# First scores, first loads and first mixing rewritten in a blockwise attention and MLP-mixer kernel

## The chip, the cores and the metric

The kernel runs on one core of one Trainium2 chip. A core has a matrix engine (TensorE, PE), a vector engine (VectorE, DVE), a scalar engine (ScalarE, ACT), a general one (GpSimd, POOL) and a queue engine (SyncE, SP). Each takes its own instructions strictly in the order of its queue and waits on semaphores for the others. Loads and stores are issued by an engine and carried out by 16 DMA engines which all the queues share. The metric is the time of one execution in microseconds (us).

## The reference

There are 8 batches of 8 heads, 576 positions and 64 elements per head; all inputs and outputs are float32.

```python
scores = np.matmul(q, k.transpose(0, 1, 3, 2)) / np.sqrt(64)
scores = np.where(i // 64 >= j // 64, scores, -1e9)         # causal in blocks of 64
attn = exp(scores - max); attn = attn / (sum(attn) + 1e-9)
x = concat_heads(attn @ v)                                  # (8, 576, 512)
h = np.maximum(x^T @ w_tok1, 0) @ w_tok2                    # mixes positions, 576 -> 256 -> 576
u = x + h^T
out = u + np.maximum(u @ w_ch1, 0) @ w_ch2                  # mixes channels, 512 -> 1536 -> 512
```

## The kernel before

**How work is ordered.** The kernel first describes its work as operations, `P.add(engines, cost, emit, ...)`. An operation is a small group of instructions of one engine (a group of matmuls into one PSUM bank, a load, an exponential) and gets the next number. The string `ORDER` (from line 100) then lists all of them by hand: a number, the letter of the engine (T = PE, A = ACT, D = DVE, P = POOL, S = SP), and the letters of the PSUM banks that the operation takes (a to h; s and t are the pair banks of the first scores). `placed()` emits them in that order, so that ORDER is, engine by engine, the queue that runs. Costs and priorities beside an operation play no part any more. Semaphores between the engines follow from the tiles that are read and written.

**A batch.** Four heads of one k or q (a "first" and a "second" half of the heads, hg 0 and 1) are one load of 128 partitions by 1152 elements. From the second batch on, and for all values and weights, POOL's queue loads them and casts them to bf16 on the way (L418 for k and q, L468 for the values). DVE turns them with 32x32 stream transposes, two per load (L442). PE then makes scores (L568), ACT their exponentials (L587 for the first batch, L774 for others), POOL, DVE or ACT copy tails (L596) and clear blocks (L601), PE multiplies by the values (L618, L638), and DVE divides by the row sums (L644). That gives x. Token mixing is `token_up` (L809, relu at L795 or L797), then for every 128 positions products with w_tok2 (L904), a DVE add of x (L919) which gives u as rows, four PE transposes (L991) and an evacuation of them (L1007 by ACT, L1009 by DVE), which gives u as columns (`uT`). Channel mixing is `channel_up` (L1032) and `channel_down_fast` (L1366), a product of blocks with fewer multiplications, which needs sums and differences of weight blocks made by DVE (`weight_sums`, L1318, for w_ch2; `up_weight_sums`, L1063, for w_ch1), and which ends in `fold`: DVE adds the residual u (L1412) and SyncE stores the rows (L1457). The last 64 positions of all batches are put together at the end as one more batch.

**The start of the first batch.** `load_qk(0, 0)` brings the first heads in four halves, (0, 9) and (9, 18) of 18 groups of 64 elements: both halves of k and the first of q are loaded by SyncE as float32 into `stage` (space in `gT`) and cast to bf16 by ACT (L400) or DVE (L402); the second half of q comes in two casting loads by POOL's queue, groups 9 to 14 and 14 to 18 (L437). `load_qk(0, 1)` brings the second heads by POOL in two halves for q and two for k. `init_tiles` fills constants (L344): ones and zeros of the two value tiles, the zero rows of w_tok1 and of its odd copy `w1o_sb`. `raise_clock` gives PE matmuls on zeros while nothing else is there: 11 of 512 columns and up to 110 of 256 columns (ORDER takes them with T).

**The order of POOL's loads before.** Two q pieces; second heads' q, then k, in halves; batch 1's k of the first heads; five pieces of the first heads' values; batch 1's q; one piece of the second heads' values; w_tok2; four more value pieces with batch 1's second k between them; w_tok1 in three; batch 1's second q; one piece of w_ch1; batch 2's first q; the other seven of w_ch1 (L502); batch 2's first k; the values of batch 1; batch 2's second k and q; w_ch2 in three (L511).

**First batch's mixing before.** `first_uT` makes the columns of u directly. For each 128 channels, four matmuls of x with the identity (L842) put x^T into a bank and two matmuls of 512 columns (L857) add the mixing; one evacuation by ACT or DVE (L872, L874) gives `uT`. The rows of u, which `fold` needs, are made later by `turn`: four times four matmuls of `uT` with the identity (L1388) and a cast (L400 or L402).

```python
    ORDER = """
    13S 22P 24P 5P 9D 2D 3P 16S 44Ta 12P 19S 10P 4P 30P 14D 15D 17A 32P 1D 26P 18D 20A 28P 0A 45Tb 23D 25D 21D 252P 46Tb
```

Of the kernel before, what the change touches and what calls it, by code (L numbers as in the profile page):

```python
# [27 lines left out]
class Plan:  # L28
# [19 lines left out]
    def __init__(self):  # L48
        self.ops = []
        self.free = {}  # L50
# [4 lines left out]
    def add(  # L55
        self, engines, cost, emit, deps=(), prio=0.0, take=(), give=(), xfer=None, mode=0, at=0.0,
        urgent=0, until=1e9, quick=False, stick=False,
# [10 lines left out]
        o.n = len(self.ops)  # L68
        self.ops.append(o)
# [5 lines left out]
    def placed(self):  # L75
# [21 lines left out]
        assert all(o.n in done or o.until < 1e9 for o in self.ops)  # L97
# [3 lines left out]
    13S 22P 24P 5P 9D 2D 3P 16S 44Ta 12P 19S 10P 4P 30P 14D 15D 17A 32P 1D 26P 18D 20A 28P 0A 45Tb 23D 25D 21D 252P 46Tb  # L101
    47Tb 48Tb 49Ta 50Ta 37P 51Ta 52Ta 53Ta 54Ta 55Ta 56Ta 35P 57Ta 7D 174Tst 175T 34P 195A 58Ta 59Ta 60Ta
    61Ta 196A 62Ta 38P 197D 63Ta 31D 64Ta 65Ta 66Ta 176A 199Tt 36P 177A 178D 67Ta 179D 68Ta 33D 69Ta 255P 70Ta 200A
    180Ts 27D 198P 71Ta 72Ta 40P 73Ta 181A 29D 182Tt 157P 74Ta 75Ta 76Ta 183A 77Ta 201Ts 43P 78Ta 79Ta 80Ta 253D
    202A 42P 214Tt 254D 188Tb 189T 41P 215A 184Tc 11D 233Ts 6D 190D 191D 258P 192Td 211Ta 234A 220Tt 216P 256D 39P
    185T 257D 221A 81Tb 218Ts 155P 212D 213D 207Tb 235D 208T 186D 219A 158P 187D 237Tt 193D 209D 156P 203Ta 210D
    204T 238A 194D 239Ts 261P 205D 206D 164P 8D 240A 236D 269Tcbda 424P 271A 163P 281Tefgh 270A 166P 259D 273A 217D
    226Tb 283A 227T 284A 222Tc 223T 228D 241Ta 242T 282A 229D 165P 249Tf 224D 245Tg 285A 225D 162P 246T 230Tb 243D
    244D 339Tc 159P 250D 231D 232D 337Ta 251D 247D 161P 340A 260D 272A 276Tbfeh 338D 348Tc 262D 160P 278A 349T 263D
    345Ta 280A 346T 248D 277A 341Td 350D 421P 301Tgbfh 274D 347D 264P 343Tc 342D 303A 275D 351Ta 304A 265P 352T 344D  # L110
    305A 425D 354Td 355T 302A 313Tcbfh 279A 356D 306P 387Tg 353A 267P 426D 384Td 315A 388T 266P 316A 404Ta 385T 317A
    268P 408Tb 314A 381Te 386D 405A 416Tf 427P 409D 390Tc 389A 307P 391T 333D 430P 372Td 392A 308Tabhg 167P 373T
    311A 334D 382T 168P 310A 369Tc 309A 370T 169P 417A 375Tb 335D 434P 312A 378Ta 379T 383A 433P 366Th 374A 367T
    422D 371A 436P 400Td 423D 376T 380A 289Tc 377A 295Ta 290D 298Tf 368A 291D 330Tb 296D 401A 297D 292Tc 299D 286Tg
    331D 332D 438Tadeh 300D 287D 293D 288D 324Tb 440A 294D 357Tf 325D 439A 321Tc 326D 363Tg 428D 442A 364T 322D 441A
    323D 450Tbdah 431D 365A 318Tc 429D 454A 358T 453A 319D 327Te 432D 360Tg 451A 320D 361T 452A 328D 329D 482Tcabh
    362A 443D 359D 502Te 444P 483A 435P 393D 485A 604P 484A 504Td 503A 437P 170D 486A 470Tcbag 595P 505A 171D 601P
    473A 445Tfehd 471A 172D 514Ta 448A 508Tc 472A 173D 515A 512Th 506Tb 446A 509D 510Ta 474A 513D 397Tcf 447A 475P
    507D 449A 476P 394D 598P 477Tbghe 398A 403Td 395D 480A 479A 511D 481A 493Th 396D 520Ta 478A 490Tg 518Te 521A
    494D 407T 406D 519A 495D 597D 464Ta 596D 455Te 461Th 410D 458Tb 399T 465D 491D 456D 457D 462D 459D 466D 411T  # L120
    463D 600D 402D 496Ta 522Te 412D 516Th 413T 523A 497D 599D 419S 517A 460D 762P 492D 499Te 414D 759P 467Tb
    612Thgcd 498D 526D 415T 336D 615A 616A 614A 530Tca 613A 487Td 500D 468D 469D 531Tg 533A 501D 617P 527D 545Thb
    532A 418D 618P 536T 611P 548A 524Te 488D 489D 534Tg 537A 525D 610P 551T 528D 535A 624Tdecf 605D 608P 552A 538T
    606D 628A 607P 540T 529D 627A 539D 678Th 626A 609P 603D 625A 549Tc 602D 679A 619Tdfge 541D 550A 546Th 622A 760D
    553T 623A 763D 543T 620A 547D 676Tg 621A 761D 544A 644Tdehf 542D 926P 677A 554D 555T 647A 764D 560Tag 648A 556D
    561Tc 929P 563A 680Th 557D 765P 562A 684Tf 681D 645A 566T 558T 685D 646A 564Tc 567A 649D 559D 651Tdhef 650P 565A
    768P 638Ta 653A 635Tb 772P 639D 568T 652A 640D 570T 636D 654A 637D 686Ta 569D 655A 656Tbdhe 571D 641Tc 660A 687D
    629Tf 659A 573T 642D 630D 689S 643D 632Ta 658A 631D 682Te 572D 657A 788Tcfdh 633D 634D 574A 673Tb 683D 790A
    670Ta 674D 789A 664Tg 688S 675D 671D 579Tef 672D 791A 665D 792A 666D 769D 783Tbagc 580A 667Td 784A 661Th 668D
# [45 lines left out]
    1473T 1472D 1381A 1411D 1477S 1534T 1531D 1474D 1574Tbc 1570D 1554Tag 1535D 1575A 1571D 1475T 1555A 1550D 1537D  # L175
    1576T 1539D 1540T 1476D 1551D 1478S 1580T 1552D 1542T 1541D 1547S 1578Td 1546S 1543D 1560T 1572D 1544T 1573D
    1581D 1553D 1558Th 1561D 1545D 1564T 1579D 1548S 1549A 1559D 1584T 1565D 1582T 1577D 1585D 1566T 1589A 1583D
    1556T 1588A 1567D 1562T 1569S 1557D 1586T 1563D 1568S 1587D 1590S
"""


# [1385 lines left out]
```

## Time and profile before

| | us |
|---|---|
| median of 3 runs | 284.15 |
| lowest and highest | 283.65, 284.55 |
| the profiled execution | 284.69 |
| its span, first to last instruction | 282.9 |
| PE: first scores | 8.30 |
| ACT: exponentials of the first batch | 9.06 to 21.32 |
| PE: first channel-up product | 32.14 |
| PE: first scores of the third batch | 43.69 |
| PE: first down product | 55.75 |

A row of the profile's timeline or of its chain of waits reads "start, length, engine, line, operation, output<-input, count", and in brackets the idle time of the engine before it with what ended it. `x9` stands for nine instructions drawn together. A row of the groups of instructions has busy time and mean nanoseconds of one behind the first bar. In the DMA view a queue's row gives packets, MB and its packets' time as a share, and an issue's row the size of one and the median time from issue to landing. q0 is POOL's queue, q1 SyncE's. All times count from the start of the span; 1.8 us of the execution lie outside of it.

The granted clock of PE has a mean of 1.0 over the span.

### The profile page before, as it was taken

The page shows a single profiled execution, that of the slowest core. Times are in us where ns is not written, and L with a number is a line of the kernel's source. Part 1 is how long each engine was busy: PE and PEld are TensorE (multiplying, and loading weights), DVE is VectorE, ACT ScalarE, POOL GpSimd, SP SyncE. Part 2 cuts the span into 40 slices and gives each one's busy share as a digit, 9 for nine tenths or more (in the row PEclk, how much of TensorE's full clock was granted, in tenths as well). Part 3 has the DMA queues.
Part 4 walks back from the last instruction along what each step waited for, and adds up shares of the span by engine and source line. Part 5 has one row for each costly group of instructions (what it writes and reads, how often), then busy time and mean ns, then how long its engine had stood idle before and what let it go on. Part 6 is the DMA issues. An engine that isn't in the chain of part 4 may idle for free.

```text
span 282.9 us, 9352 instructions
## 1 busy us (share of the span) xinstructions
PE 275.3 (97%) x3982; PEld 204.0 (72%) x3982; DVE 238.9 (84%) x515; ACT 179.2 (63%) x331; POOL 72.7 (26%) x126
## 2 busy tenths in 40 slices
PE   7899999999999999999999999999999999999994
PEld 3466556588776788986877658756789876568884
DVE  3688669999889998999998979859896997579984
ACT  3798788953998856897879866274533744652200
POOL 8895870511631351063232221000000000000000
PEclk9999999999999999999999999999999999999999
DMA  7999999954979492999598594100044502200157
GB/s 163 160 178 192 202 190 206 152 92 86 142 87 139 87 150 56 250 109 170 66 118 139 56 188 60 70 10 19 0 84 95 196 0 76 75 1 2 74 151 224
DMA packets 64890, 31.95 MB, mean 113 GB/s; under 512 B 53200, under 2 KB 55888, under 8 KB 64848
## 3 DMA queue, kind: packets, MB, share of 16 engines
q0 software_dynamic: 44896, 17.49, 53.6%
q1 hardware_dynamic: 19520, 13.21, 18.2%
q8 instruction: 31, 0.51, 0.7%
q10 hardware_dynamic: 432, 0.66, 0.7%
q14 instruction: 11, 0.09, 0.1%
HBM read 35.85 MB, written 9.44 MB: 160 GB/s over the span
## 4 chain that ended last, share of the span: by engine, by line
PE 87%; DMA 4%; ACT 3%; POOL 3%; DVE 1%; issue 1%; POOLq 0%; DVEq 0%
PE late L1366 23%; PE mm L1105 8%; PE mm L1232 7%; PE mm L1366 7%; PE late L1232 6%; PE mm L568 6%; PE late L1105 6%; DMA qk_sb<-in_k_dram 4%; PE mm L618 4%; PE mm L809 3%; PE mm L904 2%; PE late L904 2%; PE late L618 2%; PE mm L1032 2%; ACT e_sb L774 2%; PE late L809 2%
## 5 line engine op out<-in xcount | busy, mean ns | idle before, releaser
L774 ACT ACTIVATE e_sb<-mm 128x512 bf16<-128x512 f32 x82 | 46.6, 606 | 13.1 <-PE late L568 9.4
L774 ACT ACTIVATE e_sb<-late 128x512 bf16<-128x512 f32 x86 | 48.5, 609 | 9.0 <-PE late L568 8.2
L442 DVE STREAM_TRANSPOSE qk_sb<-qk_sb 128x288 int32<-128x288 int32 (+1 forms) x65 | 41.8, 694 | 4.9 <-DMA qk_sb<-in_q_dram 1.8
L468 POOL DMA_DIRECT2D vals<-in_v_dram x45 | 36.9, 832 | 4.5 <-PE mm L618 2.4
L1366 PEld LDWEIGHTS <-gT 128*128 128x128 bf16 x336 | 32.0, 98 | 5.6 <-issue 0.4
L1366 PEld LDWEIGHTS <-sums 128*128 128x128 bf16 x324 | 31.3, 98 | 5.3 <-issue 0.4
L568 PEld LDWEIGHTS <-qk_sb 32*64 32x64 bf16 (+1 forms) x1152 | 19.0, 103 | 14.8 <-issue 11.1
L568 PE MATMUL mm<-qk_sb 32*64 32x64 bf16 (+7 forms) x504 | 26.9, 277 | 0.1
L618 PEld LDWEIGHTS <-e_sb 128*128 128x128 bf16 x640 | 23.1, 97 | 5.3 <-issue 2.2
L568 PE MATMUL late<-qk_sb 32*64 32x64 bf16 (+7 forms) x504 | 26.2, 283 | 0.6 <-issue 0.3
L1366 PE MATMUL late<-wd_sb,gT 128*128 128x256 bf16 x168 | 20.7, 273 | 0.0
L1366 PE MATMUL late<-wd_sb,sums 128*128 128x256 bf16 x168 | 20.6, 273 | 0.0
L1105 PEld LDWEIGHTS <-ws_sb 128*128 128x128 bf16 x192 | 18.2, 98 | 3.1 <-issue 0.9
L618 PE MATMUL mm<-vals,e_sb 128*128 128x65 bf16 x450 | 19.8, 193 | 0.5 <-DMA vals<-in_v_dram 0.3
L644 DVE TENSOR_TENSOR x_sb<-mm,rinv 128x256 bf16<-128x256 f32 x45 | 18.7, 422 | 1.3
L1412 DVE TENSOR_TENSOR o_sb<-late,u_sb 128x512 f32<-128x512 f32 x22 | 15.0, 684 | 3.6 <-PE late L1366 3.6
L1232 PEld LDWEIGHTS <-ws_sb 128*128 128x128 bf16 x120 | 11.7, 98 | 8.6 <-issue 0.2
L1105 PEld LDWEIGHTS <-wc_sb 128*128 128x128 bf16 x144 | 15.3, 114 | 1.5 <-issue 0.4
L1366 PE MATMUL late<-wc_sb,gT 128*128 128x256 bf16 x132 | 16.2, 273 | 0.0
L596 POOL COPY vals<-e_sb 128x256 bf16<-128x256 bf16 (+1 forms) x11 | 4.3, 393 | 39.7 <-ACT e_sb L774 39.6
L400 ACT COPY mm<-late 128x512 f32<-128x512 f32 (+1 forms) x16 | 9.1, 570 | 8.1 <-PE late L1232 5.4
L795 ACT ACTIVATE gT<-mm 128x512 bf16<-128x512 f32 x21 | 12.6, 616 | 1.9 <-PE mm L1105 0.9
(198 smaller groups left out, 630.7 us busy)
## 6 DMA issues: line engine op xcount, KB each, us to landing
out_dram<-o_sb SPq DMA_DIRECT2D x19, 256.0 KB, 3.0
qk_sb<-in_k_dram POOLq DMA_DIRECT2D x14, 288.0 KB, 6.0
qk_sb<-in_q_dram POOLq DMA_DIRECT2D x14, 288.0 KB, 5.9
vals<-in_v_dram POOLq DMA_DIRECT2D x28, 128.0 KB, 4.5
out_dram<-o_sb SPq DMA_DIRECT2D x7, 512.0 KB, 3.8
wc_sb<-in_moe_w_ch_dram POOLq DMA_DIRECT2D x8, 192.0 KB, 7.5
wc_sb<-in_moe_w_ch_dram POOLq DMA_DIRECT2D x3, 512.0 KB, 10.5
vals<-in_v_dram POOLq DMA_DIRECT2D x15, 64.0 KB, 5.3
```

The lines of the kernel that those rows point to most:

```text
L442: nc.vector.transpose(dst[:, 0:S, :] .rearrange("p s e -> p (s e)") .bitcast(I32) .rearrange("p (a k) -> p k a", k=NB)[:, k0:k1], raw2.bit ...
L468: nc.gpsimd.dma_start(out=t[128 - p : 128, J, hs, 0:64], in_=src)
L568: nc.tensor.matmul(out=home(n)[rows, c : c + w], lhsT=bar[r, 0] if j is None else kT[i][r, keys, par], rhs=bar[r, 1] if j is None else qT[ ...
L618: nc.tensor.matmul(out=u[:, I, 0:65], lhsT=e[:, h, c : c + 128], rhs=vt[:, J, head, 0:65], start=(J == 0), stop=(J == I),)
L644: nc.vector.tensor_tensor(out=xt[:, 0:4, 64 * head : 64 * head + 64], in0=u[:, :, 0:64], in1=ri[:, 0:4].to_broadcast([128, 4, 64]), op=MULT,)
L774: nc.scalar.activation(dst, bank_of(x), EXP, scale=scale)
L795: nc.scalar.activation(dst, src, RELU)
L809: nc.tensor.matmul(out=ps, lhsT=w1_sb[:, c, tt : tt + 255 : 2], rhs=xt[:, c, cols], start=(c == 0), stop=False)
L1105: nc.tensor.matmul(out=bank_of(bank)[:, 256 * o_ : 256 * o_ + 256], lhsT=x(o_, m), rhs=y[:, :, m, :], start=opens, stop=m == 1, skip_group ...
L1232: nc.tensor.matmul(out=bank_of(bank)[:, 128 * c : 128 * (c + step)], lhsT=x(m), rhs=y[:, c : c + step, m, :], start=opens, stop=m == 1, sk ...
L1366: nc.tensor.matmul(out=bank_of(bank)[:, 256 * i : 256 * i + 256], lhsT=x[:, kk, 128 * i : 128 * i + 128], rhs=y[:, kk], start=first and i ...
L1412: nc.vector.tensor_tensor(out=dst, in0=src, in1=other, op=ADD)
```

## The change

It has these parts.

1. The second half of the first heads' q is loaded by SyncE as float32 and cast by ACT, as the other three halves are, and turned by one stream transpose, not two.
2. The second heads' q and k of the first batch come in one POOL load each, cast on the way, not in two.
3. Two fills move from DVE to POOL, ahead of its loads: the zero rows of the second value tile and those of `w1o_sb`.
4. POOL's loads have another order: second heads' q, then k; the five value pieces of the first heads; batch 1's k, then q, of the first heads; the five value pieces of the second heads; w_tok1 in three; w_tok2; batch 1's k, then q, of the second heads; w_ch1 in eight; batch 1's values; batch 2's k and q of the first heads; k and q of the second; w_ch2 in three.
5. The first batch's mixing goes by rows, as in the other batches: for each half of the channels and each 256 positions, four matmuls of 256 columns, a DVE add of x (now u as rows), four transposes, an evacuation. `turn` goes, since the rows are there. These operations are numbered from 2000 on.
6. The first 24 of PE's fillers on zeros are two matmuls of 128 columns, not one of 256.
7. The first batch's upper half of rows is stored by one DMA, not two.
8. The early part of ORDER is written anew. Operations from 25 on have a number one lower. From the second batch's token mixing on (about 55 us), each engine's operations are the same in the same order, with other PSUM banks. Earlier, besides the above: two relus of the first batch's token_up pass from DVE to ACT, one of the second batch's from ACT to DVE, four evacuations of the first channel-up swap between ACT and DVE, and some tail copies between POOL and DVE.

```diff
 def add(..., later=False):
-        o.n = len(self.ops)
+        if later:
+            o.n, self.later = self.later, self.later + 1
+        else:
+            o.n, self.count = self.count, self.count + 1
 ...
 ORDER = """
-    13S 22P 24P 5P 9D 2D 3P 16S 44Ta 12P 19S 10P 4P 30P 14D 15D 17A 32P 1D 26P 18D 20A 28P 0A 45Tb 23D 25D 21D 252P 46Tb
-    47Tb 48Tb 49Ta 50Ta 37P 51Ta 52Ta 53Ta 54Ta 55Ta 56Ta 35P 57Ta 7D 174Tst 175T 34P 195A 58Ta 59Ta 60Ta
+    13S 5P 9D 2D 3P 16S 43Ta 12P 19S 22S 10P 4P 6P 11P 29P 14D 15D 17A 1D 25P 18D 20A 23A 0A 44Tb 21D 24D 36P 45Tb 46Tb
+    47Tb 48Ta 49Ta 34P 50Ta 51Ta 52Ta 53Ta 54Ta 55Ta 33P 56Ta 7D 173Tst 174T 37P 194A 57Ta 58Ta 59Ta 60Ta 195A 61Ta 35P
 ...
-    WARM, KEEP = 11, 110
+    WARM, KEEP, HALVED = 11, 110, 24
 ...
         for i in range(2):
+            fill("POOL", ("v", i), -1e6 + i, (v1[i][0:64, 4, :, :], 0.0))
             fill(
                 ("POOL", "DVE")[i], ("v", i), (-1e6, -40)[i],
-                (v1[i][0:64, 4, :, :], 0.0),
 ...
-        fill("DVE", "w1", -1e5 + 3, (w1o_sb[0:64, :], 0.0))
+        fill("POOL", "w1", -9e5 + 1, (w1o_sb[0:64, :], 0.0))
 ...
-            if not first:
+            if b or hg:
 ...
-            edges = (0, 9, 18) if not (first and n) or hg else (0, 9, 14, 18)
+            edges = (0, 9, 18)
             for f, (k0, k1) in enumerate(zip(edges, edges[1:])):
-                if first and not hg and n + f < 2:
+                if first and not hg:
 ...
-    def first_uT(x_done, a_done, w2_ready):
+    def first_uT(a_done, w2_ready):
+        xt, at, ut = x_sb[0], aT[0], u_sb[0]
+        done, rows = [], {}
+        P.count += 3 * NDM
+        for f in range(2):
+            cols = slice(256 * f, 256 * f + 256)
+            for p in range(2):
+                def emit(o, p=p, cols=cols, bank=bank):
+                    for i in range(2):
+                        for t in range(NDT):
+                            si = 2 * p + i
+                            nc.tensor.matmul(
+                                out=bank_of(bank)[:, 256 * i : 256 * i + 256],
+                                lhsT=w2_sb[:, t, 128 * si : 128 * si + 128], rhs=at[:, t, cols],
+                                start=i == 0 and t == 0, stop=t == NDT - 1, skip_group_check=i > 0,
+                            )
 ...
+                    nc.vector.tensor_tensor(
+                        out=ut[:, 2 * p : 2 * p + 2, cols],
+                        in0=bank_of(bank).rearrange("p (t c) -> p t c", c=256),
+                        in1=xt[:, 2 * p : 2 * p + 2, cols], op=ADD,
+                    )
 ...
+                    ps = bank_of(bank).bitcast(BF16)[:, 0:512]
+                    for i in range(2):
+                        for m in range(2):
+                            nc.tensor.transpose(
+                                ps[:, 256 * i + 128 * m : 256 * i + 128 * m + 128],
+                                ut[:, 2 * p + i, 256 * f + 128 * m : 256 * f + 128 * m + 128], ident,
+                            )
 ...
+                    dst = uT[0][:, 2 * p : 2 * p + 2, 2 * f : 2 * f + 2, :]
 ...
+        return done, rows
 ...
-                rows_done = u_done if b else [turn(row, col)] if residual else []
+                if b == 0:
+                    P.count += 2 * residual
+                    rows_done = [u_done[row, col]] if residual else []
+                else:
+                    rows_done = u_done
 ...
-                    step = 1 if row == 0 else nt
+                    step = 1 if row == 0 and b else nt
```

More of the change, by code (lines that the diff above doesn't have):

```diff
@@ L48, in __init__ @@
     def __init__(self):
-        self.ops = []
+        self.ops = {}
+        self.count, self.later = 0, 2000
         self.free = {}
@@ L56, in add @@
         self, engines, cost, emit, deps=(), prio=0.0, take=(), give=(), xfer=None, mode=0, at=0.0,
-        urgent=0, until=1e9, quick=False, stick=False,
+        urgent=0, until=1e9, quick=False, stick=False, later=False,
     ):
@@ L435, in load_qk @@
                 elif first:
-                    def emit_load(o, k0=k0, k1=k1, hbm=hbm, raw2=raw2):
-                        nc.gpsimd.dma_start(out=raw2[:, D * k0 : D * k1], in_=hbm[:, D * k0 : D * k1])
-                    loads = [P.add("POOL", 0.69 if not hg and f == 1 else 0.55, emit_load, (), -1e4 + n + 4 * hg, xfer=0.084 * (k1 - k0) + 0.3 * (not hg and f == 1))]
+                    P.count += f
                 def emit(o, raw2=raw2, dst=dst, k0=k0, k1=k1):
@@ L892, in token_mix @@
             ]
[L893 removed]
+            done, u_done = first_uT(a_all, w2_ready)
             prio = 0.5
```

255 lines of the change are left out of this document (117 added, 138 removed).

## The prediction

> **What bounds the kernel now.** I read the page's shares first, then the chain of work that ended last, then the timeline of each engine up to 60 us, and last the DMA view in short windows, since the change touches nothing later: from the second batch's token mixing on (about 55 us) both orders name the same operations in the same sequence on every engine.
>
> ```profile
> PE 275.3 (97%) x3982; PEld 204.0 (72%) x3982; DVE 238.9 (84%) x515; ACT 179.2 (63%) x331; POOL 72.7 (26%) x126
> PE 87%; DMA 4%; ACT 3%; POOL 3%; DVE 1%; issue 1%; POOLq 0%; DVEq 0%
> 6.63 6.33 DMA qk_sb<-in_k_dram
> 15.86 6.03 DMA qk_sb<-in_k_dram
> 21.98 0.72 DVE qk_sb L442
> 45.01 1.57 ACT e_sb L774 x3
> ```
>
> The first two rows are TensorE's busy share and the chain by engine: late in the run PE alone sets the end, so whatever PE gains by 60 us should stay gained. The other four are rows of the chain (start, length, what): before 23 us it runs through POOL's loads, not through PE, and from 45 to 52 us through ScalarE's exponentials. So the early part has three limits in turn, and a saving on PE alone is not automatically a saving.
>
> **The start.** The first scores need all of the first k and q.
>
> ```profile
> gT<-in_k_dram SPq DMA_DIRECT2D x2, 288.0 KB, 3.0
> gT<-in_q_dram SPq DMA_DIRECT2D x1, 288.0 KB, 5.1
> q1 hardware_dynamic: 213, 0.43, 93.3%
> q1 hardware_dynamic: 97, 0.20, 53.9%
> q0 software_dynamic: 133, 0.07, 51.0%
> 6.82 0.67 ACT L400 CAST qk_sb<-gT 128x576 bf16<-128x576 f32 x1 [1.77 <-DMA gT<-in_q_dram]
> 6.60 1.65 DVE L442 STREAM_TRANSPOSE qk_sb<-qk_sb 128x160 int32<-128x160 int32 x3 [0.80 <-DMA qk_sb<-in_q_dram]
> 8.30 0.51 PE L568 MATMUL sc<-qk_sb 32*64 32x192 bf16 x28 [1.53 <-DVE qk_sb L442]
> ```
>
> Rows one and two: issue to landing of SyncE's loads; the k halves took 3.0 us, the q half 5.1. Rows three to five are the queues (packets, MB, share) in 2.50-3.75 us and 3.75-5.00 us: alone, SyncE's queue moved 0.43 MB in 1.25 us, 0.34 MB per us; once POOL's queue joined it fell to 0.20 MB. With POOL's q pieces gone, SyncE's four halves (1.18 MB) have the engines to themselves until POOL's next load moves. By 3.75 us it has moved 0.58 MB, so the other 0.60 MB need about 1.75 us, to 5.5, and I allow 0.5 us to landing (the two k halves' last bytes moved near 3.9 us, their cast began at 4.37): third half 5.15, fourth 6.0. Two ScalarE casts of 0.67 us end at 6.7, one stream transpose of 0.7 (the last of the three in row seven) at 7.45, instead of 8.25 now. PE starts its scores at 7.45: **0.85 us earlier**. Bounds: if the last half takes 3.2 us from its issue at 2.1 it is 1.4 us earlier; if both q halves queue as the one does now (6.82, then 0.68 more) the scores start at 8.95, 0.65 later. The middle is nearer the undisturbed rows, so I take it.
>
> ```profile
> 9.06 7.09 ACT L587 ACTIVATE e_sb<-sc 128x384 bf16<-128x384 f32 x9 [1.47 <-PE sc L568]
> 16.39 4.93 ACT L587 ACTIVATE e_sb<-sc 128x1024 bf16<-128x1024 f32 x5 [0.23 <-PE sc L568]
> ```
>
> From 9.06 to 21.32 ScalarE runs batch 0's exponentials with one gap of 0.23 us, so the 0.85 us passes through to 20.45, if the second heads' k and q are there.
>
> **POOL's queue.** POOL drops two q pieces and loads the second heads' q and k in two issues, not four, but gains two fills ahead of them.
>
> ```profile
> 1.25 1.24 POOL L437 DMA_DIRECT2D qk_sb<-in_q_dram  x2 [0.80 <-POOLq L1551]
> 4.52 1.08 POOL L437 DMA_DIRECT2D qk_sb<-in_q_dram  x2
> 7.15 3.65 POOL L468 DMA_DIRECT2D vals<-in_v_dram  x5
> L344 POOL MEMSET vals<- 64x528 bf16 x1 | 0.5, 532 | 0.1
> L344 POOL MEMSET w_sb<- 64x256 bf16 x1 | 0.6, 591 | 0.1
> 13.24 0.54 POOL L479 DMA_DIRECT2D w_sb<-in_moe_w_tok_dram  x1 [0.70 <-DMA qk_sb<-in_k_dram]
> ```
>
> The two q issues of the first row (1.24 us) go, fills of 0.53 and 0.59 us come, so the second heads' q is issued near 4.5 as now (4.52); two issues of 0.54 us fewer let the values follow near 5.5 instead of at 7.15, the more so as batch 1's k goes behind them. The last row is a back-pressure: the fifteenth load waited for the seventh (6.63 + 6.33 = 12.96), so POOL keeps eight loads in flight and from 12 us on is paced by landings. Through that queue I count 288 KB of bf16 per k or q load: k of batch 1's second heads now lands at 21.88 and its transpose (21.98) sits in DVE's queue ahead of the clear that PE's head products wait for:
>
> ```profile
> 21.37 0.63 PE L568 MATMUL late<-qk_sb 32*128 32x512 bf16 x8 [0.30 <-ACT e_sb L587]
> 22.28 0.45 PE L618 MATMUL mm<-vals,e_sb 128*128 128x65 bf16 x9 [0.28 <-DMA vals<-in_v_dram]
> 22.93 0.81 PE L618 MATMUL mm<-vals,e_sb 128*128 128x65 bf16 x21 [0.21 <-DVE e_sb L601]
> ```
>
> In the new order the values and w_tok1 come first (the values near 18 us instead of 22.3) and the clears stand before that transpose, so the 0.35 us before each of the last two rows goes: **0.7 us**. What is late next: that k itself. Behind the values, w_tok1 and w_tok2 it lands near 23.2, q near 24.4, and DVE reaches the k transpose at 22.6; the wait of 0.6 us holds the head divisions and a relu queued behind it on DVE, and PE's third score set behind those. I charge **0.55 us** (0 if k lands by 22.6, 1.4 if at 24).
>
> **First batch's mixing.** Before: 16 moving matmuls of 128 columns with the identity, 8 of 512, four evacuations, and later four "turns" of 4 matmuls with four casts. After: 16 of 256, four adds, 16 transposes, four evacuations.
>
> ```profile
> 33.46 0.39 PE L1388 MATMUL mm<-ident,uT 128*128 128x128 bf16 x4
> 33.68 0.59 PE L1032 MATMUL mm<-uT,wc_sb 128*128 128x512 bf16 x2
> L919 DVE TENSOR_TENSOR u_sb<-mm,x_sb 128x512 bf16<-128x512 f32 x13 | 8.7, 684 | 1.3 <-PE mm L904 1.3
> L1009 DVE COPY umT<-late x1: 425/425/425, 72.6 to 72.6; 128x512 bf16<-128x512 bf16 x1
> L874 DVE CAST uT<-mm 128x512 bf16<-128x512 f32 x3 | 2.0, 681 | 0.3 <-PE mm L857 0.3
> L400 ACT CAST u_sb<-mm 128x512 bf16<-128x512 f32 x2 | 1.3, 642 | 0.0
> ```
>
> A turn holds PE for 33.68 - 33.46 = 0.22 us; the 4096 mixing columns stay and the identity matmuls become transposes of the same width, so PE loses four turns: **0.88 us**. DVE gets four adds of 0.68 and four copies of 0.43 (4.4 us) for three casts of uT and one of u (2.7 us); ScalarE loses one uT and three u casts (2.5 us) and takes over two 256-column relus. New waits: each group of transposes waits for its add, and on PE the next mixing products, channel-up products and scores stand behind it. By my walk through the new order that leaves PE waiting some 0.3 us in three places before 31 us, already within the figure below. The single merged store of batch 0 is issued near 66 us beside dense PE work: nothing; without that cover one 0.6 us issue. Halved clock fillers stream the same columns: nothing, bounded by their 0.11 us each.
>
> Sum to batch 2's first scores: 0.85 + 0.7 + 0.88 - 0.55 = **1.9 us** earlier on PE.
>
> **What caps it.** The next load that matters is w_ch2, for whose sums the first down products wait.
>
> ```profile
> q0 software_dynamic: 15086, 8.20, 121.1%
> 38.16 0.53 POOL L511 DMA_DIRECT2D wc_sb<-in_moe_w_ch_dram  x1 [0.36 <-DMA vals<-in_v_dram]
> wc_sb<-in_moe_w_ch_dram POOLq DMA_DIRECT2D x1, 512.0 KB, 12.2
> 50.80 1.82 DVE L1318 TENSOR_TENSOR wd_sb<-wc_sb 128x1536 bf16<-128x1536 bf16 x2
> 54.66 0.69 DVE L919 TENSOR_TENSOR u_sb<-mm,x_sb 128x512 bf16<-128x512 f32 x1 [0.18 <-PE mm L904]
> 58.34 0.68 DVE L919 TENSOR_TENSOR u_sb<-mm,x_sb 128x512 bf16<-128x512 f32 x1
> 59.36 0.39 PE L991 MATMUL mm<-ident,u_sb 128*128 128x128 bf16 x4
> ```
>
> The last third lands at 38.16 + 12.2 = 50.4; DVE starts the sums at 50.80, only 0.4 us later. After the change POOL's queue holds the same loads up to there, less 144 KB (the q pieces), issued from the same 4.5 us, but its engines stand idle for some 0.8 us after SyncE's loads where now POOL's pieces move. The first row is POOL's queue from 0 to 50 us: 8.20 MB, from 3.5 us on, are 176 KB per us, at which 144 KB take 0.8 us: the two nearly cancel. I take the landing at 50.1 (49.5 to 50.8). The sums then start at 50.15, 0.65 us earlier; DVE's 0.18 us wait at 54.66 goes, and PE's transposes at 59.36 have 0.36 us of slack behind DVE's add (58.34 + 0.61). So DVE lets PE be at most 0.65 + 0.18 + 0.36 = **1.2 us** earlier. The smaller of 1.9 and 1.2 decides, and PE is dense behind it.
>
> The profiled execution took 284.69 us with a span of 282.9; less 1.2 it is 283.5. It lies 0.54 above the median of 284.15, so in medians 284.15 - 1.2 = 283.0.
>
> **Rivals.**
>
> The cap doesn't bind: w_ch2 lands before 49.4. For it: whole k and q loads are longer rows. Against: halves landed as fast per byte as whole ones. PE's 1.9 us then counts, up to 2.4 with the k wait gone: 282.0.
>
> The q halves land no earlier: two queues take the engines in turn, as the 0.20 MB row shows. Start 0.65 later instead of 0.85 earlier; 1.9 - 1.5 = 0.4 us remain, under the cap: 283.75. The Trainium skill says the same in "DMA: Bandwidth & Descriptors", section "Rules for kernel authors": spreading DMAs over SP, ACT and GpSimd gives no bandwidth, since all run on the same 16 engines, and only saves issue time. By that rule the sum loses its 0.85 us; the trace agrees on the sharing, but here the sharing partner is gone.
>
> Slower, by one mechanism: eight in flight at five small value loads and three of w_tok1 in a row.
>
> ```profile
> vals<-in_v_dram POOLq DMA_DIRECT2D x9, 64.0 KB, 5.5
> q0 software_dynamic: 2031, 1.04, 121.1%
> ```
>
> Eight times 64 KB per 5.5 us is 93 KB per us; 288 KB of values would take 3.1 us instead of 1.6 at the mean of 176, w_tok1's pieces, by estimate, 0.5 more, and w_ch2 would land at 52.2. The sums start 1.4 us later than now, less the 0.54 us of slack 0.86 later: 285.0. It costs from a landing of 51.3 on. For it: today big loads stand between the small ones. Against: the second row is POOL's queue from 6 to 13 us, with five value loads in flight among larger ones: 1.04 MB in 7 us, 149 KB per us. The Trainium skill's "DMA: Bandwidth & Descriptors", section "Anatomy of one DMA", fits 2.0 us plus bytes at 436 GB/s, an estimate of 2.15 us for 64 KB, by which eight in flight would not throttle; the rows say 5.5, and they decide.
>
> **Chances.** Forecast 0.45 (its own range 282.3 to 283.7), no cap 0.22, late q 0.18, small loads 0.15. About 0.3%, 0.85 us, is what a measurement of this kernel tells from no change, so faster means under 283.3: 0.45 x 0.72 + 0.22 + 0.03 = 0.57; slower, over 285.0 or just there, 0.14; the rest 0.29. The range 281.8 to 284.6 leaves out most of the last case and the best tail of the second.
>
> **What would show it.** PE's first scores at 7.4 to 7.6; exponentials ending near 20.5; no wait on values near 22, but a DVE wait for in_k near 22.6; no L1388 rows; w_ch2's last third landing near 50.1 with a DVE wait ahead of L1318. Wrong if scores start after 8.3, if L1318 starts later than 50.8, or if PE shows new idle time after 60 us: the new PSUM homes would then cost, which I set at nothing, since order and releasers stay.

## The result, and the profile after

The changed kernel took 286.09 us in the median of 6 runs (285.21 to 286.58), the kernel before 284.15 beside it. One of its six runs there, at 289.23 us, was in a slow state, and medians and ratios here leave such runs out. The ratio is 1.0062, with a 95% interval of 1.0039 to 1.0084: about 1.8 us **slower**, where 1.2 us faster was forecast. The profiled execution took 286.58 us with a span of 284.8; that of before has 282.9.

The shares and the chain by engine, from the page of the changed kernel:

```profile
PE 274.2 (96%) x3979; PEld 205.5 (72%) x3998; DVE 239.1 (84%) x513; ACT 178.5 (63%) x329; POOL 71.8 (25%) x126
PE 72%; DVE 10%; DMA 9%; POOL 5%; issue 2%; ACT 1%; SPq 0%; DVEq 0%; POOLq 0%
```

PE had 87% of the chain before and has 72% now, and DVE went from 1% to 10%. So the chain now passes through DVE more often. These shares do not tell where time is lost: after_homes, a run below that loses nothing from 66 to 271 us, has 77% and 7%.

Rows of the timeline of the changed kernel up to 51 us (start, length, instruction, and in brackets the idle time ahead of it with its releaser):

```profile
3.26 0.69 POOL L421 DMA_DIRECT2D qk_sb<-in_q_dram  x1
7.55 0.51 PE L568 MATMUL sc<-qk_sb 32*64 32x192 bf16 x28 [0.86 <-DVE qk_sb L442]
19.88 0.43 PE L568 MATMUL mm<-qk_sb 32*64 32x320 bf16 x2 [0.39 <-DVE x_sb L699]
24.09 0.72 DVE L442 STREAM_TRANSPOSE qk_sb<-qk_sb 128x288 int32<-128x288 int32 x1 [1.75 <-DMA qk_sb<-in_k_dram]
25.68 0.36 PE L568 MATMUL mm<-qk_sb 32*64 32x448 bf16 x1 [1.27 <-DVE aT L797]
50.03 1.82 DVE L1343 TENSOR_TENSOR wd_sb<-wc_sb 128x1536 bf16<-128x1536 bf16 x2
```

The first scores start at 7.55 (8.30 before). POOL issues its first load at 3.26, not at the forecast 4.5. DVE stands 1.75 us for batch 1's k and PE 1.27 us behind DVE's relu. The w_ch2 sums start at 50.03 (50.80 before), with no DMA wait ahead of them.

The start of one and the same matmul in both traces says more than shares do. Paired that way, PE is 1.32 us ahead of the kernel before at 66 us, almost exactly the forecast 1.2. Then it loses this bit by bit: 0.92 ahead at 117, 0.50 at 161, 0.08 at 173, and 0.64 **behind** at 186. From there to 271 us nothing changes. Between 66 and 186 us both kernels run the same operations in the same order; only the PSUM banks differ. A word of ORDER (a number, an engine and the letters of banks) says into which bank a group of PE's matmuls writes, and by the kernel's semaphores the group may start only when the last instruction that reads that bank has ended. PE's waits from 66 to 190 us (engine, tile, line, releaser: total, times, longest), which the same view of the kernel before does not have at all:

```profile
PE mm L1257 <- DVE x_sb L644: 0.5, 1, 0.5
PE mm L929 <- DVE x_sb L644: 0.2, 1, 0.2
```

The larger one in the timeline, first the kernel before and then the changed one:

```profile
179.31 0.42 DVE L644 TENSOR_TENSOR x_sb<-mm,rinv 128x256 bf16<-128x256 f32 x1
181.68 1.03 PE L1232 MATMUL mm<-uT,wc_sb 128*128 128x512 bf16 x4
181.93 0.76 DVE L644 TENSOR_TENSOR x_sb<-mm,rinv 128x256 bf16<-128x256 f32 x2
184.06 0.60 PE L1232 MATMUL late<-uT,wc_sb 128*128 128x256 bf16 x4
```

```profile
181.70 0.59 PE L1257 MATMUL late<-uT,wc_sb 128*128 128x512 bf16 x2
182.75 0.59 PE L1257 MATMUL mm<-uT,wc_sb 128*128 128x512 bf16 x2 [0.46 <-DVE x_sb L644]
182.27 0.76 DVE L644 TENSOR_TENSOR x_sb<-mm,rinv 128x256 bf16<-128x256 f32 x2
184.69 0.60 PE L1257 MATMUL mm<-uT,wc_sb 128*128 128x256 bf16 x4
```

The four channel-up products start level (181.68 and 181.70). Before, all four run through: by the kernel's own tiles and semaphores, their second bank was released at 179.75 by an earlier head division (first row). After, the second pair is given the bank that the division at 182.27 is still reading; that read ends at 182.71 and PE goes on at 182.75. The last rows of the two fences are the same matmuls 2.4 us later: the 0.02 us has become 0.63. At 163.7 us it is the same: a bank given back by an add at 163.28 before, one given back by a division at 163.51 after. Other steps, 0.06 to 0.15 us each at 70, 89, 107, 121, 124, 138, 159, 168 and 176 us, are under what the waits view lists.

At the end 1.2 us more are lost: the 0.64 at 271 us grow to 1.86 in the span. The DMA view of before and of after from 262 us on, the 512 KB store of the last full rows, with the median from issue to landing:

```profile
out_dram<-o_sb SPq DMA_DIRECT2D x1, 512.0 KB, 2.8
```

```profile
out_dram<-o_sb SPq DMA_DIRECT2D x1, 512.0 KB, 4.8
```

```profile
274.38 0.42 DVE L1415 TENSOR_TENSOR o_sb<-late,e_sb 128x256 f32<-128x256 f32 x1 [0.64 <-DMA out_dram<-o_sb]
```

The last row is DVE in the changed kernel: a fold that reuses the store's rows waits 0.64 us for it, and PE's lag grows from 0.64 to 1.1. The rest lies behind PE's last matmul: 0.34 up to the last landing, and 0.42 behind it. From the last landing to the end pass 1.05 us before and 1.47 after; in both, SyncE's 80th instruction starts 0.48 us after its 79th. Before, with one store instruction more on that queue, this stand falls into the wait for the last store; after, it comes behind it.

### The profile page after: what moved, and what is told of

It is laid out like the page before. It is cut to its first block, busy times and chain, and to the rows that moved or that the text cites. A ratio compares the mean times of both kernels' runs of the same rounds, so it can differ in the third digit from the quotient of the medians.

```text
span 284.8 us, 9337 instructions
## 1 busy us (share of the span) xinstructions
PE 274.2 (96%) x3979; PEld 205.5 (72%) x3998; DVE 239.1 (84%) x513; ACT 178.5 (63%) x329; POOL 71.8 (25%) x126
## 4 chain that ended last, share of the span: by engine, by line
PE 72%; DVE 10%; DMA 9%; POOL 5%; issue 2%; ACT 1%; SPq 0%; DVEq 0%; POOLq 0%
PE late L1391 15%; PE mm L1391 8%; PE mm L1257 7%; PE late L1130 7%; PE mm L1130 6%; PE late L1257 5%; DMA qk_sb<-in_k_dram 5%; PE mm L568 4%; DMA wc_sb<-in_moe_w_ch_dram 3%; POOL vals L468 3%; PE mm L618 3%; PE late L568 2%; DVE o_sb L1415 2%; PE late L618 2%; PE mm L809 2%
## 5 line engine op out<-in xcount | busy, mean ns | idle before, releaser
L774 ACT ACTIVATE e_sb<-mm 128x512 bf16<-128x512 f32 x94 | 53.7, 608 | 12.0 <-PE mm L568 6.0
L774 ACT ACTIVATE e_sb<-late 128x512 bf16<-128x512 f32 x74 | 43.2, 605 | 11.7 <-PE mm L568 7.0
L442 DVE STREAM_TRANSPOSE qk_sb<-qk_sb 128x288 int32<-128x288 int32 x64 | 41.7, 701 | 5.4 <-DMA qk_sb<-in_k_dram 4.3
L568 PE MATMUL mm<-qk_sb 32*64 32x128 bf16 (+7 forms) x556 | 27.7, 280 | 1.9 <-DVE aT L797 1.3
L568 PE MATMUL late<-qk_sb 32*64 32x128 bf16 (+7 forms) x452 | 26.6, 279 | 0.2
L618 PEld LDWEIGHTS <-e_sb 128*128 128x128 bf16 x640 | 23.2, 97 | 4.3 <-issue 2.4
L1130 PEld LDWEIGHTS <-wc_sb 128*128 128x128 bf16 x144 | 15.3, 114 | 1.4 <-issue 0.4
L1391 PE MATMUL late<-wd_sb,sums 128*128 128x256 bf16 x126 | 15.6, 273 | 0.0
L795 ACT ACTIVATE gT<-late 128x512 bf16<-128x512 f32 x21 | 12.7, 609 | 3.6 <-PE late L1257 2.4
L1391 PE MATMUL late<-wd_sb,gT 128*128 128x256 bf16 x120 | 14.8, 273 | 0.0
L421 POOL DMA_DIRECT2D qk_sb<-in_q_dram x15 | 8.4, 558 | 24.7 <-DVE x_sb L644 14.6
L1257 PEld LDWEIGHTS <-wc_sb 128*128 128x128 bf16 x90 | 10.0, 113 | 5.6 <-issue 0.7
```

The costliest lines, as they stand in the source:

```text
L421: nc.gpsimd.dma_start(out=raw2, in_=hbm)
L442: nc.vector.transpose(dst[:, 0:S, :] .rearrange("p s e -> p (s e)") .bitcast(I32) .rearrange("p (a k) -> p k a", k=NB)[:, k0:k1], raw2.bit ...
L568: nc.tensor.matmul(out=home(n)[rows, c : c + w], lhsT=bar[r, 0] if j is None else kT[i][r, keys, par], rhs=bar[r, 1] if j is None else qT[ ...
L618: nc.tensor.matmul(out=u[:, I, 0:65], lhsT=e[:, h, c : c + 128], rhs=vt[:, J, head, 0:65], start=(J == 0), stop=(J == I),)
L774: nc.scalar.activation(dst, bank_of(x), EXP, scale=scale)
L795: nc.scalar.activation(dst, src, RELU)
```

## The experiments

**The theory** after this: the new banks cost some 2 us between 66 and 186 us, because some words are given a bank that comes free just in time. **The rivals**: the early stalls and the cap by w_ch2 set the time; the halved fillers or the merged store do; or one is looking at a drift between executions. The table has all runs. "Lead" is how much earlier than in the first profile of the kernel before the same PE matmul starts (a minus: later), at 66, 173 and 271 us; "scores" is PE's first score. The runs were made in four later sessions; each ratio is against the kernel before in the same session, whose medians were 284.35 to 284.54.

| run | scores | lead 66 | lead 173 | lead 271 | span | median | ratio, 95% interval |
|---|---|---|---|---|---|---|---|
| changed kernel | 7.55 | 1.32 | 0.08 | -0.64 | 284.8 | 286.09 | 1.0062, 1.0039 to 1.0084 |
| again | 8.15 | 0.98 | -0.25 | -0.96 | 284.4 | 286.47 | 1.0069, 1.0041 to 1.0098 |
| after_homes | 7.59 | 1.74 | 1.73 | 1.73 | 282.2 | 284.12 | 0.9996, 0.9979 to 1.0013 |
| before_homes | 7.87 | -0.76 | -2.06 | -2.82 | 285.7 | 286.48 | 1.0082, 1.005 to 1.0114 |
| late_homes | 7.63 | 1.23 | -0.16 | -0.60 | 284.4 | 285.92 | 1.0055, 1.0026 to 1.0084 |
| unmerged | 8.24 | 0.56 | 0.42 | 0.42 | 283.9 | 285.39 | 1.0033, 1.0013 to 1.0052 |
| whole_fill | 7.99 | 1.04 | 1.04 | 1.04 | 282.3 | 284.14 | 0.9993, 0.9977 to 1.001 |
| both | 8.15 | 0.39 | 0.39 | 0.38 | 283.2 | 285.31 | 1.0026, 0.9997 to 1.0056 |
| fill8 | 8.14 | 0.42 | 0.41 | 0.42 | 283.0 | 285.24 | 1.0024, 1.0006 to 1.0043 |
| mended | 8.12 | 0.87 | 0.86 | 0.87 | 281.8 | 283.99 | 0.9981, 0.9953 to 1.0009 |
| k_first | 8.29 | 0.87 | 0.87 | 0.87 | 281.9 | 283.33 | 0.996, 0.9938 to 0.9981 |
| late_pool | 7.48 | 0.32 | 0.31 | 0.31 | 282.5 | 284.46 | 0.9999, 0.9978 to 1.002 |
| before_2 | 8.00 | 0.82 | 0.81 | 0.82 | 282.0 | 283.82 | single run |

Read the columns before the ratios. The four rows with the changed kernel's banks from 55 us on, or from there to 172 us (changed kernel, again, before_homes, late_homes), lose 1.8 to 2.1 us; every other one keeps its lead within 0.02 us over 200 us, unmerged within 0.14.

**The changed kernel again.** No edit.

> The changed kernel once more, unchanged, for a second profile. In the first one PE led the kernel before by 1.32 us at 66 us and was 0.64 us behind it at 185 us. Banks (the new PSUM homes make PE wait for other releases between 70 and 185 us): the lead is lost again at the same places, 1.3 at 66 us to about 0.3 to 0.7 behind at 185 us, time 285.7 to 286.5. Chance (stalls at random places): the lead is lost elsewhere or not at all, and the time differs from 286.1 by over 0.5. Engines (DVE or ACT cannot be earlier): the lead goes to 0 at 185 us but not below.

The same result, and the same places: lead 0.98 at 66 us and -0.96 at 271. The loss from 66 to 271 us is 1.94, against 1.96. But the early part varies: its first scores start at 8.15, not 7.55.

**The banks of before in the changed kernel.** 203 words of ORDER from about 55 us on get the bank letters that the kernel before has there, up to a renaming of letters; no operation moves. Some of them:

```diff
-463Td
+463Ta
...
-495Tg
+495Ta
...
-913Ta
+913Th
```

> The changed kernel up to 55 us; from there on the operations take the PSUM banks of the kernel before, up to a renaming of banks. Banks: the lead of 1.3 us at 66 us is still there at 185 us, time 284.2 - 1.3 = 282.9 (282.5 to 283.5). Engines: the lead is lost all the same to DVE and ACT, 284.2 to 284.7. Chance: 285.5 to 286.5, as the changed kernel.

The lead of 1.74 us stays to 271 us without loss, and the median is 2.35 us under that of the changed kernel run beside it (284.12 against 286.47). This is the cause of the loss between 66 and 186 us. The four channel-up products that stood at 182 us run through:

```profile
179.95 1.03 PE L1258 MATMUL mm<-uT,wc_sb 128*128 128x512 bf16 x4
```

The run also shows that a lead of 1.74 at 66 us is to be had: the cap of 1.2 does not hold.

**The banks of the changed kernel in the kernel before.** The same exchange the other way; the early part stays that of before.

```diff
-464Ta
+464Tb
...
-496Ta
+496Th
```

> The kernel before up to 55 us; from there on the operations take the PSUM banks of the changed kernel, up to a renaming. Banks: it loses between 70 and 185 us what the changed kernel lost there, up to 2.0 us: 285.3 to 286.2. Engines and chance: 284.0 to 284.6, no difference.

Nothing of the change but its banks, and 2.3 us slower in ratio (0.0082 of 284.54). PE's waits from 66 to 190 us:

```profile
PE mm L1231 <- DVE x_sb L643: 0.3, 1, 0.3
PE mm L903 <- DVE x_sb L643: 0.2, 1, 0.2
```

They are the two waits of the changed kernel: the same products and the same head division under this kernel's line numbers. The lead falls by 2.06 between 66 and 271 us.

A caution on the view by windows. PE's busy time from 66 to 120 and from 160 to 190 us, first in the kernel before, then in the changed one, then in after_homes (window, then length, PE busy with its instructions, clock, DMA share, GB/s):

```profile
66.00:120.00 54.00, 54.00 (x961) 1.00 1.00 129
...
160.00:190.00 30.00, 30.00 (x425) 1.00 0.50 85
```

```profile
66.00:120.00 54.00, 53.35 (x984) 1.00 1.01 131
...
160.00:190.00 30.00, 29.13 (x389) 1.00 0.57 86
```

```profile
66.00:120.00 54.00, 53.39 (x991) 1.00 0.98 132
...
160.00:190.00 30.00, 29.84 (x380) 1.00 0.51 82
```

From 66 to 120 us the changed kernel seems to have 0.65 us of new idle time, but after_homes has 0.61 of it too and loses nothing there. Only the second window tells them apart: 0.87 us idle against 0.16. Matmuls overlap, and the trace's ends of them are modelled, so pair the starts.

**The banks of before from 172 us on only.** 65 words, from the operation at 172 us to the end.

```diff
-913Ta
+913Te
...
-1158Td
+1158Tf
```

> The changed kernel in full, but from about 172 us on its PSUM words take the banks that the kernel before gave them. Theory (each loss of PE lies at a place where a word is given a bank that comes free just in time): up to 172 us the lead over the kernel before is lost as in the changed kernel, from about 1.0 to 1.3 us at 66 us to about 0 at 172 us; the steps of 0.10 at 175.7 us and of 0.46 to 0.62 us at 182 us are gone, and the time is 285.4 to 285.8. Rival (a wait that is taken away in one place comes back at the next tight one): the lag at 185 us is +0.5 to +0.7 us as in the changed kernel, and the time is 286.1 to 286.5.

Half a hit for each side. Up to 172 us the lead is lost as in the changed kernel (1.23 to -0.16), and the wait at 182 us is gone. But where the two sets of banks meet, a new one has come:

```profile
PE late L1392 <- ACT e_sb L775: 0.3, 1, 0.3
PE mm L930 <- DVE x_sb L645: 0.2, 1, 0.2
```

The first of the two is new, at 173.6 us, and takes 0.44 us of the lead. From 173 us on the same 0.44, against 0.72 in the changed kernel, is all that is lost, and the median of 285.92 lies 0.1 above the range of the theory and within the interval of the changed kernel. So the waits belong to single words, but a word cannot be mended by itself: its bank is taken from another.

**Two stores again for batch 0's upper rows**, on top of after_homes.

```diff
-                    step = 1 if row == 0 and b else nt
+                    step = 1 if row == 0 else nt
```

> The changed kernel with the banks of before, and batch 0's upper rows stored in two DMAs again, not one, so that SyncE has as many instructions as in the kernel before. End theory: in the changed kernel 1.45 us lie between the landing of the last store and the end of the span, against 1.05 before, since SyncE stands 0.47 us ahead of its final drain; the stall is tied to the place of that instruction in SyncE's program, so with one instruction more it falls into the wait for the store: 1.05 us again, time 0.4 less than with the banks alone (284.1), 283.7. Rival (a store's landing varies by itself): 1.45 stays, 284.1.

Slower than after_homes, 285.39 against 284.12, and than whole_fill in its own session (284.14), and not only at the end. Its lead is 0.57 at 48 us already, long before the first store of batch 0 is issued (65.60). From the last landing to the end pass 1.85 us: two more instructions on SyncE, and the last store's semaphore waited for first. That is 0.4 us; the other 0.9 is not explained.

**Whole fillers**, on top of after_homes.

```diff
-    WARM, KEEP, HALVED = 11, 110, 24
+    WARM, KEEP, HALVED = 11, 110, 0
```

> The changed kernel with the banks of before, and PE's first 24 fillers whole again, so PE has 24 matmuls fewer. End theory: the fetch of PE's instructions (one packet of 16 KB) at about 270 us then comes some 2.6 us later and no longer beside the store of 512 KB, which lands in 2.8 us instead of 4.6, so that the fold's wait of 0.41 us on out_dram ahead of DVE's L1415 goes: time 0.25 to 0.5 less than 284.1. Rival (halved fillers keep the start shorter): scores start up to 0.1 later, no gain at the end: 284.1 to 284.2.

The 512 KB store lands after 2.8 us and DVE does not wait at 274 us. Still the median stays (284.14 against 284.12): the lead at 66 us is 0.7 smaller in the profile. So the trace shows what goes with the halved fillers at the end, and the medians show no net effect.

**Both edits**, on top of after_homes.

> The changed kernel with the banks of before, two stores and whole fillers. End theory: the lead of 1.3 to 1.7 us at 260 us reaches the end but for 0.2: 284.1 - 0.4 - 0.4 = 283.3 (283.0 to 283.6), faster than the kernel before. Rival: 284.1.

285.31, like unmerged alone (285.39), with a lead of 0.39. In both runs with two stores the median is 1.2 us up, whole fillers or not.

**Eight idle matmuls of 256 columns on PE at 34 us**, on top of after_homes. They go into a bank that nobody reads.

```diff
 372T
+81Tb 82Tb 83Tb 84Tb 85Tb 86Tb 87Tb 88Tb
 333D
```

> The changed kernel with the banks of before, and eight idle matmuls of 256 columns (0.88 us of PE) among the first batch's channel-up products at 34 us. Cap (DVE's queue, not PE, sets when PE gets on at 50 to 60 us): PE's lead at 66 us and the time stay within 0.2 of the run without them, 284.1 to 284.3. Rival (PE alone counts): the lead is 0.88 us smaller, 285.0.

Against after_homes PE is 0.72 us late at 32 us, ahead of the addition (its scores had started 0.55 later), 1.59 behind it and 1.32 at 60 us. So of the 0.87 us added 0.60 comes through to 60 us; the rest is a wait that after_homes alone has, 0.23 us for DVE at 41.70. The median is 1.1 us above whole_fill in the same session. PE's own work counts there. The run by itself does not refute a cap at 1.2, since without the addition its lead would have been 1.0 to 1.3. The pairing does: in every profile, at leads from -0.76 to 1.74, the lead at 48 us, before the w_ch2 sums begin, is that at 66 us within 0.01, so nothing in between holds PE back.

**Mended end**: whole fillers, and the store of operation 1588 by SyncE instead of ScalarE, on top of after_homes.

```diff
-1588A
+1588S
```

> The changed kernel with the banks of before and whole fillers; and one store of the last batch is issued by SyncE, not ScalarE, so that SyncE has two instructions more at its end. End theory, mended: SyncE stands some 0.48 us between its 79th and 80th instruction, whatever these are; with two more the stall falls into the wait for a store, 1.05 us lie between the last landing and the end, not 1.48, and the time is 0.4 less than with whole fillers alone (284.1): 283.7, faster than the kernel before. Rival (the end varies by itself, or the store is later on SyncE): 284.0 to 284.5.

From the last landing to the end pass 0.92 us instead of 1.47 in whole_fill, the span is the shortest of all (281.8), and the median 283.99. Its interval still includes no change.

**Batch 1's second k ahead of w_tok2**, on top of mended, to take the 1.27 us wait away.

```diff
-156P 257P
+257P 156P
```

> As the run labelled mended, and POOL loads batch 1's second k before w_tok2, not after it. PE waited 1.27 us at 24.4 us behind DVE, which waited 1.75 us for that k (landing 24.07). If PE's waits count (the forecast charged 0.55 for this one): k lands near 22.7, PE's lead at 30 us and at 66 us is 0.7 to 1.2 us larger, time 0.7 to 1.2 less. Cap (DVE and w_ch2 set when PE gets on at 50 to 60 us): the lead at 30 us is larger, at 66 us it is not over 1.4, time 0 to 0.4 less.

PE's waits from 15 to 34 us in the timeline, of mended and then of k_first:

```profile
20.67 0.43 PE L569 MATMUL mm<-qk_sb 32*64 32x320 bf16 x2 [0.52 <-DVE x_sb L700]
26.14 0.35 PE L569 MATMUL mm<-qk_sb 32*64 32x448 bf16 x1 [0.94 <-DVE aT L798]
```

```profile
20.62 0.43 PE L569 MATMUL mm<-qk_sb 32*64 32x320 bf16 x2 [0.39 <-DVE x_sb L700]
22.79 0.41 PE L619 MATMUL late<-vals,e_sb 128*128 128x65 bf16 x8 [0.49 <-issue]
```

DVE's transposes that wait, of mended and then of k_first:

```profile
24.56 0.72 DVE L443 STREAM_TRANSPOSE qk_sb<-qk_sb 128x288 int32<-128x288 int32 x1 [1.49 <-DMA qk_sb<-in_k_dram]
```

```profile
25.86 0.72 DVE L443 STREAM_TRANSPOSE qk_sb<-qk_sb 128x288 int32<-128x288 int32 x1 [0.67 <-DMA qk_sb<-in_q_dram]
```

PE's wait at 26 us is gone, a smaller one of 0.49 stands at 22.8, and DVE waits 0.67 us for q instead of 1.49 for k. The median, 283.33 or a ratio of 0.996, is the one that beats the kernel before with its whole interval. Against mended the gain of 0.66 us is not certain: the intervals overlap, and the leads at 66 us are equal in the two profiles, though k_first's scores started 0.17 later. Paired with mended, it is 0.6 us ahead at 26 us, and nothing of that is left at 30.

**POOL's first load later**, on top of mended: one fill is made five times over, so that the load goes at 4.9 us, near where the prediction had it.

```diff
-                    (nc.vector if engine == "DVE" else nc.gpsimd).memset(t, value)
+                    for _ in range(5 if prio == -9e5 + 1 else 1):
+                        (nc.vector if engine == "DVE" else nc.gpsimd).memset(t, value)
```

> As the run labelled mended, and POOL fills one block five times over, some 1.2 us, before its first load, which then is issued at 4.5 us, not at 3.26. If POOL's early load takes the engines from SyncE's last two halves (they landed at 5.3 to 6.0 and 6.05 to 6.7 in seven profiles): they land at 5.2 and 5.9 and the scores start at 7.4 to 7.6; everything that POOL loads is up to 1.2 us later. Rival (SyncE's halves queue behind each other anyway): scores at 7.9 to 8.2 as without it.

The timeline of late_pool:

```profile
4.91 0.69 POOL L423 DMA_DIRECT2D qk_sb<-in_q_dram  x1
5.12 2.31 DVE L444 STREAM_TRANSPOSE qk_sb<-qk_sb 128x288 int32<-128x288 int32 x3
5.27 1.40 ACT L405 CAST qk_sb<-gT 128x576 bf16<-128x576 f32 x2 [0.19 <-DMA gT<-in_q_dram]
```

And of the changed kernel run again, where POOL's first load goes at 3.26:

```profile
6.04 1.31 ACT L403 CAST qk_sb<-gT 128x576 bf16<-128x576 f32 x2 [1.09 <-DMA gT<-in_q_dram]
```

With SyncE's loads alone on the DMA engines the first q cast starts at 5.27 instead of 6.04, and the scores at 7.48 instead of 8.15, as forecast for this state. But it is one profile, and three of the ten with the early load (changed kernel, after_homes, late_homes) start at 7.55 to 7.63 too. The lead at 66 us is 0.32 here, against 0.87 in mended: in this one profile the 1.65 us on POOL's queue cost more than the 0.64 at the start brings, and the medians (284.46 against 283.99) have overlapping intervals.

**The kernel before, profiled again.** No edit.

> The kernel before, unchanged, for a second profile. Scores started at 8.30 us in the first one. If the start varies as in the changed kernel (7.55 to 8.24 in seven profiles), they start anywhere from 7.8 to 8.4; the stall of SyncE lies between the same two instructions and the store of 512 KB lands in 2.8 us.

Its scores start at 8.00 and it is 0.82 us ahead of its own first profile at 66 us. The part before 66 us varies by this much from execution to execution, so a lead there is known only as a mean.

## Why the prediction was wrong

**The step that failed** is the one behind the cap: "PE is dense behind it", so that what PE gains by 60 us stays, with the PSUM homes put at nothing "since order and releasers stay". The order stayed; the releasers did not. A word's bank decides which instruction must have read it last, and a word with another bank has another releaser. The homes cost 1.94 and 1.96 us in two profiles of the changed kernel, 2.06 in the kernel before, and none in after_homes. The prediction named "new idle time after 60 us" as what would show it wrong, but gave it neither a price nor a chance among its rivals. Up to there the forecast was near: the lead at 66 us was 1.32 in the first profile and 1.0 in the mean of eight, 1.2 by forecast.

That it was near is largely luck. By its terms:

- **The start**, 0.85: mis-sized. In ten profiles with the changed start and POOL's first load at 3.3 us the first scores lie at 7.55 to 8.29, mean 7.99; in three of the kernel before at 7.87 to 8.30, mean 8.06. It gains 0.07. The step said that POOL's next load goes at 4.5, since two fills of 0.53 and 0.59 us would take the place of two issues of 1.24. But without those issues the fills began at 0.75 and not at 2.53, and the load went at 3.26. Its packets moved from 5.0 to 5.3 us on. By 5.25 us SyncE's queue was further along in the three early starts (0.54 to 0.55 MB since 3.75 us, third half landed at 5.30 to 5.40) than in the other seven (0.46 to 0.52 MB, landed at 5.78 to 6.07), where POOL's packets could still get in its way. That fits the sharing that the second rival had, by another partner, and late_pool agrees, with a start at 7.48 against the forecast 7.45. That the sharing is the cause is argued, not shown. The Trainium skill's "DMA: Bandwidth & Descriptors", section "Issuing engines are not separate DMA queues", says of this that loads of different engines interleave on the same 16 DMA engines. The trace of the kernel before agrees, where SyncE's queue fell from 0.43 to 0.20 MB in 1.25 us as POOL's joined it. By that rule alone the 0.85 would have been left out.
- **The stalls near 22 us**, 0.7: the two waits are gone, as expected, but the rows from which the text took 0.35 each show 0.28 and 0.21, and they are no fixed cost: in before_2 neither is there, in before_homes PE waits 1.5 us for values at 15 and 23 us.
- **The k wait**, 0.55: near in the mean. k landed at 24.07, not near 23.2. The text had 1.4 for a landing at 24; PE waits 1.27 there, and 0.39 at 19.88, which the text did not have. In nine profiles with this order of loads and the early load at 3.3 the landing lies at 23.42 to 25.02 and PE's wait at 0.12 to 1.48, mean 0.76.
- **The four turns**, 0.88: no row of L1388 is left; that PE work before 60 us counts is shown by fill8. This term carries the sum: PE's idle time from its first score to 48 us is 0.88 to 2.41, mean 1.50, in the three profiles of the kernel before, and 1.29 to 2.10, mean 1.59, in those nine. The waits that went were made up by others, and start, waits and turns as measured give 0.07 - 0.09 + 0.88 = 0.86 of the mean lead of 1.0.
- **The cap**, 1.2: fell. The sums started at 50.03, as worked out (50.15), but the landing did not hold them. Their first half waits for two thirds, landed by 48.07, and the second half started at 50.90, behind the last third's 50.51: DVE's own queue set their start. In all eleven profiles with the changed early part the sums start 0.55 or 0.56 us less early than PE, whether its lead is 0.32 or 1.74, and that lead stands at 48 us already: the sums follow PE, and not PE the sums.
- **The halved fillers and the merged store**, nothing: at the end they cost. The store issued at 269.52 brings 0.64 us of DVE wait and 0.46 of PE lag; SyncE's stand costs 0.4 (1.47 against 1.05, and 0.92 in mended). Neither was looked for there, because the change to them stands at the start.
- **The rival of eight small loads in flight** did not come: the w_ch2 thirds landed at 45.55, 48.07 and 50.51, 0.2 later than before, not 1.8.

The mean lead at 66 us of the eight profiles with the changed early part in which no load is moved and no matmul or fill added (changed kernel, again, after_homes, late_homes, unmerged, whole_fill, both, mended) is 1.02 us; the three of the kernel before lie at 0, 0.82 and -0.76, mean 0.02. So the early edits earn about 1.0 us. The banks take 1.9 to 2.0. From 271 us to the end of the span the two profiles of the changed kernel lose 1.2 and 0.5 more. The sum is 1.4 to 2.2 us slower, with the measured 1.8 within.

What is not settled: why the two stores of unmerged and both go with 0.9 us beyond the 0.4 that they cost at the end; what SyncE stands for between its 79th and 80th instruction; and why DVE, in the two profiles of the changed kernel alone, idles ahead of the second sum at 180.8 us (row below). The semaphore of PE that the row names was up 0.22 us before the sum starts, and at DVE's other long waits for PE in these two profiles it is 0.02 to 0.09. In before_homes, late_homes and after_homes the idle time is 0.10. Since before_homes has the same banks and loses 0.46 at 182 us, not 0.62, it is worth about 0.16 there.

```profile
180.79 0.69 DVE L1220 TENSOR_TENSOR e_sb<-uT,e_sb 128x1024 bf16<-128x1024 bf16 x1 [0.46 <-PE mm L1391]
```

## What to carry to other kernels

"Same order on every engine" is not "same waits": where a scratch bank is handed from one user to the next, list for each word who frees its bank, when, and how much slack is left, and price a new assignment by the places with little slack. Swapping only the assignment between the two kernels, in both directions, settled in two runs what no reading of shares could. And look at the end of the run for every edit that changes an engine's count of instructions or stores, wherever the edit stands.

## What the hardware showed that was not expected

**A packet of instructions can hold up a store.** Queue q8 moves 16 KB packets of kind "instruction" through the run, 31 in the changed kernel. The changed kernel's DMA queues from 268 to 274 us (packets, MB, share):

```profile
q1 hardware_dynamic: 401, 0.78, 45.8%
q8 instruction: 1, 0.02, 0.9%
```

The one packet of q8 starts at 272.30 and takes 0.88 us, while the 512 KB store is moving. With 24 more matmuls in the program it falls there; without them it comes later (274.34 before, 273.63 in mended), so I take q8 for PE's. In the six profiles where it falls within the store, the store takes 4.8, 3.4, 4.6, 4.7, 4.5 and 3.6 us (changed kernel, again, after_homes, unmerged, late_homes, fill8); in all eight others it takes 2.8. That the packet is the cause is argued from this agreement; moving it alone was not tried.

The Trainium skill's "Advanced Engine Details and Errata", section "ISA Cache", has instruction lines of 16 KB, 256 instructions each. 31 lines would be 7936 instructions; the profile's page of the changed kernel counts 3979 matmuls and 3998 weight loads on PE, 7977, so the trace agrees with the size to within 1%.
